# Loading k and q two heads to a transfer over all 128 partitions, with the first stage's engine orders rewritten: a three-layer kernel on one Trainium2 core

## The chip, the cores and the metric

One core of a Trainium2 chip. The metric is device time in microseconds (us), the median of several runs; lower is better. The engines are TensorE (PE, with its weight loads listed apart as PEld), VectorE (DVE), ScalarE (ACT), GpSimd (POOL) and SyncE (SP), whose queue issues nearly all DMAs.

## The reference, cut to what matters

Three layers follow one another: a Nystrom-style attention on q, k, v of shape (4, 8, 576, 64), then two feed-forward layers of width 2048 on the 2304 x 512 result.

```python
q_lm = q.reshape(B, H, 32, S // 32, D).mean(axis=3)      # 32 landmarks
k_lm = k.reshape(B, H, 32, S // 32, D).mean(axis=3)
A, Bm, C = sm(q, k_lm), sm(q_lm, k_lm), sm(q_lm, k)      # softmax of scaled scores
Z = Bm.T / (norm1(Bm) * norminf(Bm) + 1e-6)
for _ in range(6):
    Z = 2 * Z - Z @ Bm @ Z
x = A @ Z @ C @ v
h = x @ w_in;   x = (h * cos(h)) @ w_out                 # layer 2
h = x @ w_in2;  out = (max(h,0) + alpha*min(h,0)) @ w_out2
```

## The kernel before, in words

The work is cut into named operations. Each has a context and a number (`u0:20` is the twentieth operation of unit 0), a list of engines that may run it, and buffers from which the dependences follow. A long string, ORDER, lists all 3937 operations. `Plan.go` walks it and emits each operation on the engine behind the slash (`/A` ACT, `/V` DVE, `/G` POOL) or else on the first engine of its list. So ORDER is the program order of every engine: an engine runs its own entries strictly in turn, and an entry whose input is late holds all that stand behind it. No planner is in the file, only its result.

The contexts that matter here:

- `w`: filler matmuls on PE (L533), whose result is unused.
- `u0`, `u1` (batch 0) and `U2` to `U7` (batches 1 to 3): attention units of four heads, function `unit`. Operations 1 and 2 load k and q on SP, 3 loads v. In u0 and u1, 4 and 11 reorder k and q on ACT (L675), 5 to 10 and 12 to 17 transpose them in thirds on PE and copy each out (L688), 18 and 19 are the landmark sums on PE (L720), 20 and 21 scale them into `kq` (L727), 22 to 28 are scores, maximum and exponential of C, 29 to 32 transpose that and copy it out, 33 is C times v on PE (L816) and 36 scales it. 37 is the scores of A; 38 to 49 are their softmax and split, of which 41 (L850, subtract the maximum), 46 (L855, multiply by the reciprocal sum) and 49 (L555, low part) may go to POOL or DVE. From U4 on the landmarks come from two trees of five additions each on POOL (L742).
- `z0`, `z1`, `z2`: the 32 x 32 inverse iteration, a serial chain that alternates between PE (L936) and DVE (L953). It starts with L882, which needs `kq` of both units of its batch, and ends with `wt`. `z0:20` is the first step that also needs C v of both units (`u0:36`, `u1:36`).
- `v`, `V`: layer 2's input weights multiplied by `wt` (L999); `v0` needs `wt` and w_in blocks c0 to c3.
- `c0` to `c63`: conversion of a 128 x 512 weight block on DVE (L568, L570, L572) after its load (L562, SP). w_out blocks are then split in two on ACT (L552) and POOL or DVE (L555, operation 6). Raw blocks share three buffers.
- `t0` to `t127`: layer 2 in 128 ticks. `t:1` is six matmuls (L1043), 2 to 6 are ACT, DVE, ACT, DVE, ACT (the cosine, the product, its high part), 7 the low part on POOL or DVE (L1056), 8 to 11 twelve matmuls into the accumulators (L1068). `e` copies a finished group of accumulators out (L1092) on ACT or DVE.
- `b`, `s`, `y`, `o`: layer 3, by a Strassen scheme (L1357, L1438), from about 435 us on.

The subtractions of L552 to L556, L1056 and L850 run through the helper `sub` and so stand under L410 in the profile; copies stand under L405 and L407.

The k and q loads of u0 and u1 are two DMAs of 288 KB each, each into 64 of the 128 partitions (two heads side by side in a partition). Those of U2 to U7 are four DMAs of 144 KB each, one head into 64 partitions in pieces of 256 B. SP keeps at most eight DMAs under way: from the ninth on, each waits for the landing of an earlier one.

```python
for bb in range(2):                                         # L637, u0 and u1
    nc.sync.dma_start(
        out=t.t[64 * bb:64 * bb + 64].rearrange("p (h x) -> p h x", h=2),
        in_=src[b, 4 * c + 2 * bb:4 * c + 2 * bb + 2].rearrange("h (p r) d -> p h (r d)", r=NR))
```

Of the kernel before, what the change touches and what calls it, by code (L numbers as in the profile page):

```python
# [25 lines left out]
u1:14 w:11 u1:33 z0:15 z0:16 c2:2 U2:2 u1:35 u0:38 u0:39 c1:2 z0:18 u0:40 u1:36 u0:41/V z0:20 u1:12 w:12 u0:42
u1:15/A u1:13/A z0:21 c1:3 z0:22 U2:4 w:13 u1:16 c8:1 u1:17/A U2:6/A U2:5/A u0:43 u0:44 z0:19 c2:3 z0:23 c2:4 u0:45
u0:46/V z0:24 w:14 u1:37 c9:1 z0:25 c1:4 u0:47 z0:26 U2:14 u0:48 u1:39 u1:38 z0:27 u0:49/G u1:40 w:15 z0:28 z0:29
u1:41/V z0:30 U2:13 w:16 u1:42 U2:15/A c8:2 z0:31 u1:43 z0:32 z0:33/A U2:16/A z0:34/A u1:44 c8:3 c9:2 u1:45 c8:4 v0:1
w:17 U3:1 c3:5 c2:5 c11:1 v0:2 v0:4 u1:46/V v0:3 u1:47 v0:5 c9:3 u1:48 U2:10 c9:4 u1:49/V c11:2 U2:12/A U2:11/A U2:17  # L30
# [1486 lines left out]
```

## Time and profile before

| | us |
|---|---|
| timed runs, median (lowest, highest) | 830.67 (830.56, 831.22) |
| span of the profiled execution | 827.8 |
| median less span (what lies around the span) | 2.9 |
| first matmul of tick 0, last start of a tick's first matmul | 46.9, 431.8 |

The span is the time from the first to the last instruction of the profiled execution. Busy times of different engines overlap, so they don't add up to the span. A matmul counts as busy from its start to a modelled end, so a busy PE need not run at its full pace.

### The profile page before, as it was taken

What the parts mean: (1) busy time and instruction counts of PE and PEld (TensorE: products, weight loads), DVE (VectorE), ACT (ScalarE), POOL (GpSimd) and SP (SyncE); (2) the same over time, 40 slices, a digit from 0 to 9 for tenths busy, and PEclk for the clock granted to TensorE, in tenths of its full rate; (3) what the DMA queues carried; (4) which work ended last, traced back from release to release, by engine and by line L of the source; (5) the groups of instructions that cost most, each with busy time, mean ns of one, the idle gap of its engine ahead of it and who ended that gap; (6) DMA issues with size and microseconds to landing.
All of it is one profiled execution on the core that took longest, in us unless ns stands there. A gap on an engine that the chain in (4) does not pass through costs nothing.

```text
span 827.8 us, 16875 instructions
## 1 busy us (share of the span) xinstructions
PE 805.2 (97%) x6490; PEld 717.1 (87%) x6490; DVE 610.1 (74%) x1256; ACT 419.4 (51%) x943; POOL 192.9 (23%) x217
## 2 busy tenths in 40 slices
PE   8889999999999999999999999999999999999997
PEld 6567789988788898899999888989998989999886
DVE  3999799877886867889788998765565556456653
ACT  4468655778754557567764444522433244323231
POOL 0003312435530112036621113203400133000020
PEclk9999999999999999999999999999999999999999
DMA  9985466675666864454542422221031012120231
GB/s 222 217 236 155 132 164 209 164 173 115 137 206 210 259 199 151 146 181 168 168 146 87 131 90 66 78 85 39 13 102 51 9 57 83 48 62 14 81 111 26
DMA packets 87904, 103.34 MB, mean 125 GB/s; under 512 B 35856, under 2 KB 62992, under 8 KB 87824
## 3 DMA queue, kind: packets, MB, share of 16 engines
q1 hardware_dynamic: 87744, 102.14, 43.0%
q8 instruction: 51, 0.84, 0.4%
q14 instruction: 29, 0.24, 0.1%
q10 hardware_dynamic: 80, 0.13, 0.0%
HBM read 79.96 MB, written 22.28 MB: 124 GB/s over the span
## 4 chain that ended last, share of the span: by engine, by line
PE 70%; DVE 16%; ACT 5%; DMA 4%; issue 3%; POOL 0%; SPq 0%; DVEq 0%; ACTq 0%; POOLq 0%
PE acc L1438 20%; PE acc L1068 16%; PE h L1357 10%; PE h L1043 8%; PE x L1357 7%; DVE m L410 3%; DVE m L1050 1%; PE x L999 1%; DMA m<-in_moe_w_in_dram 1%; DVE m L572 1%; DVE m L570 1%; DVE m L1053 1%; DMA m<-wi2d 1%; PE x L1402 1%; PE h L1402 1%
## 5 line engine op out<-in xcount | busy, mean ns | idle before, releaser
L410 POOL TENSOR_TENSOR m<-m,m 128x288 fp32r<-128x288 f32 (+4 forms) x154 | 147.1, 968 | 580.0 <-ACT m L1055 213.5
L1068 PE MATMUL acc<-m,m 128*128 128x288 f32 x1536 | 235.4, 299 | 0.1
L1068 PEld LDWEIGHTS acc<-m,m 128*128 128x128 f32 x1536 | 211.2, 188 | 18.7 <-issue 12.7
L1438 PE MATMUL acc<-m,m 128*128 128x512 f32 x864 | 218.0, 392 | 0.6 <-ACT m L1426 0.2
L410 DVE TENSOR_TENSOR m<-m,m 128x512 fp32r<-128x512 f32 (+4 forms) x246 | 151.5, 636 | 48.3 <-ACT m L1426 18.1
L1438 PEld LDWEIGHTS acc<-m,m 128*128 128x128 f32 x864 | 154.1, 188 | 28.4 <-DVE m L410 1.3
L1043 PE MATMUL h<-m,m 128*128 128x288 f32 x768 | 125.0, 302 | 2.5 <-DVE m L1053 1.5
L1043 PEld LDWEIGHTS h<-m,m 128*128 128x128 f32 x768 | 108.5, 190 | 8.3 <-DVE m L1053 4.6
L1357 PE MATMUL h<-m,m 128*128 128x256 f32 x768 | 108.5, 282 | 0.3 <-ACT m L405 0.2
L1357 PEld LDWEIGHTS h<-m,m 128*128 128x128 f32 x768 | 102.6, 189 | 6.3 <-ACT m L405 0.7
L1426 ACT ACTIVATE m<-m 128x512 fp32r<-128x512 f32 (+1 forms) x80 | 46.1, 585 | 92.0 <-DVE m L1424 87.4
L1052 ACT ACTIVATE m<-m,quarter 128x288 f32<-128x288 f32 x128 | 67.0, 533 | 34.5 <-DVE m L1050 33.6
L1357 PE MATMUL x<-m,m 128*128 128x256 f32 x576 | 81.7, 283 | 0.3 <-DVE m L407 0.3
L1357 PEld LDWEIGHTS x<-m,m 128*128 128x128 f32 x576 | 76.5, 189 | 4.2 <-DVE m L407 0.6
L1048 ACT ACTIVATE m<-h 128x288 int32<-128x288 f32 x128 | 51.4, 406 | 47.3 <-PE h L1043 46.4
L405 ACT ACTIVATE m<-h 128x256 f32<-128x256 f32 (+2 forms) x86 | 33.5, 392 | 81.8 <-PE h L1357 65.0
L1050 DVE SCALAR_TENSOR_TENSOR m<-h,m 128x288 f32<-128x288 f32 x128 | 57.0, 450 | 23.8 <-ACT m L1048 23.4
L1055 ACT ACTIVATE m<-m 128x288 fp32r<-128x288 f32 x128 | 55.7, 440 | 30.5 <-DVE m L1053 25.6
L1053 DVE TENSOR_TENSOR m<-m,h 128x288 f32<-128x288 f32 x128 | 56.9, 448 | 12.9 <-ACT m L1052 10.1
L1189 ACT ACTIVATE m<-m 128x512 fp32r<-128x512 f32 x68 | 41.6, 625 | 29.2 <-PE h L1357 10.5
L1380 DVE TENSOR_TENSOR m<-h,m 128x512 f32<-128x512 f32 x32 | 21.9, 686 | 32.8 <-ACT m L405 21.8
L1424 DVE SCALAR_TENSOR_TENSOR m<-m,m 128x512 f32<-128x512 f32 x64 | 45.0, 718 | 0.8
(147 smaller groups left out, 768.0 us busy)
## 6 DMA issues: line engine op xcount, KB each, us to landing
m<-in_moe_w_in_dram SPq DMA_DIRECT2D x32, 512.0 KB, 5.6
m<-wi2d SPq DMA_DIRECT2D x56, 256.0 KB, 3.0
m<-in_moe_w_out_dram SPq DMA_DIRECT2D x24, 512.0 KB, 5.2
m<-w1d SPq DMA_DIRECT2D x32, 256.0 KB, 5.4
y1d<-m SPq DMA_DIRECT2D x24, 288.0 KB, 4.4
out_dram<-m SPq DMA_DIRECT2D x35, 128.0 KB, 2.8
w1d<-m SPq DMA_DIRECT2D x16, 256.0 KB, 5.6
wi2d<-m SPq DMA_DIRECT2D x16, 256.0 KB, 3.2
```

The costliest lines, as they stand in the source:

```text
L410: ENG[e].tensor_tensor(o, a, b, op=ALU.subtract)
L1043: nc.tensor.matmul(out=hp.t[:, 0:CW], lhsT=w_[:, js], rhs=x[:, cs], start=(i == 0), stop=(i == 5))
L1048: op(act(CW, True), lambda e: nc.scalar.activation(k_.t, hp.t[:, 0:CW], AF.Copy, scale=INV2PI, bias=0.25), r=[hp], w=[k_], target=T + 0.8)
L1050: op(dve(CW), lambda e: nc.vector.scalar_tensor_tensor(u.t, hp.t[:, 0:CW], INV2PI, k_.t, op0=ALU.mult, op1=ALU.subtract), r=[hp, k_], w=[u])
L1052: op(act(CW), lambda e: nc.scalar.activation(u.t, u.t, AF.Sin, scale=2.0 * math.pi, bias=quarter), rw=[u], aset="sin")
L1053: op(dve(CW), lambda e: nc.vector.tensor_tensor(hc.t, u.t, hp.t[:, 0:CW], op=ALU.mult), r=[hp, u], w=[hc], target=T + 2.6)
L1055: op(act(CW), lambda e: nc.scalar.activation(gh.t, hc.t, AF.Copy), r=[hc], w=[gh, gl])
L1068: nc.tensor.matmul(out=yg[o].t[:, 0:CW], lhsT=w_.t[:, sl], rhs=x.t, start=(j == ja and i == 0), stop=(j == jb and i == 2),)
L1357: nc.tensor.matmul(out=rv(k), lhsT=a_.t[:, p, c2, js], rhs=b_.t[:, q_, c2, 0:hw], start=(first and c2 == 0 and i == 0), stop=(c2 == 1 and ...
L1424: op(dve(w), lambda e, m_=m_, hv=hv: nc.vector.scalar_tensor_tensor(m_.t[:, 0:w], hv(), 0.0, m_.t[:, 0:w], op0=ALU.max, op1=ALU.add), r=hr ...
L1426: op(act(w), lambda e, m_=m_, gh=gh: nc.scalar.activation(gh.t[:, 0:w], m_.t[:, 0:w], AF.Copy), r=[m_], w=[gh, gl])
L1438: nc.tensor.matmul(out=ya[n][t].t, lhsT=gv(x_), rhs=r_.t, start=(st and k == 0), stop=(en and k == 2))
```

## The change

Loads: partition 64 * bb + s now holds heads 4c + bb and 4c + 2 + bb in place of 4c + 2bb and 4c + 2bb + 1. Two neighbouring heads lie end to end in DRAM, so one DMA now reads both and writes all 128 partitions. u0 and u1 keep two DMAs of 288 KB for each of k and q; U2 to U7 have two of 288 KB in place of four of 144 KB. v is loaded in the same number of pieces and sizes from other heads. The places that read `kq`, write scores, build `wt` and multiply it swap the roles of bb and hh; the number and shapes of their instructions stay.

```diff
-                    for bb in range(2):
+                    for hh in range(2):
                         nc.sync.dma_start(
-                            out=t.t[64 * bb:64 * bb + 64].rearrange("p (h x) -> p h x", h=2),
-                            in_=src[b, 4 * c + 2 * bb:4 * c + 2 * bb + 2].rearrange("h (p r) d -> p h (r d)", r=NR),
+                            out=t.t[:, hh * NR * D:(hh + 1) * NR * D],
+                            in_=src[b, 4 * c + 2 * hh:4 * c + 2 * hh + 2].rearrange("b (p r) d -> (b p) (r d)", r=NR),
...
-                    for bb in range(2):
-                        for hh in range(2):
-                            nc.sync.dma_start(
...
+                    for hh in range(2):
+                        nc.sync.dma_start(
+                            out=f32(t.t)[:, 0:2 * NR * D].rearrange("p (r h d) -> p r h d", h=2, d=D)[:, :, hh, :],
+                            in_=src[b, 4 * c + 2 * hh:4 * c + 2 * hh + 2].rearrange("b (p r) d -> (b p) r d", r=NR),
...
-                src = v[b, 4 * c + 2 * bb:4 * c + 2 * bb + 2].rearrange("h (p r) d -> p h r d", r=NR)
+                src = v[b, 4 * c + bb:4 * c + bb + 3:2].rearrange("h (p r) d -> p h r d", r=NR)
...
-                out=dst.t[64 * bb:64 * bb + 64, 0:n],
+                out=dst.t[64 * (bb ^ swap):64 * (bb ^ swap) + 64, 0:n],
...
-                nc.tensor.matmul(out=pw[bb].t[64 * hh:64 * hh + 64, i * M:i * M + M], lhsT=y.t[sl, i], rhs=bmv()[sl, i])
+                nc.tensor.matmul(out=pw[hh].t[64 * bb:64 * bb + 64, i * M:i * M + M], lhsT=y.t[sl, i], rhs=bmv()[sl, i])
```

ORDER has the same 3937 operations. Each engine's order is new up to about tick 95; from there on PE, ACT, DVE, POOL and SP keep their old order, layer 3 included. Many slashes vanish where they named the default engine. Queues at their start:

```
SP before:   u0:1 u0:2 c3:1 u1:1 u1:2 c0:1 u0:3 u1:3 c2:1 c1:1 U2:1 U2:2 c8:1 c9:1 U3:1
SP after:    u0:1 u0:2 u1:1 c2:1 u1:2 c3:1 c1:1 u0:3 c0:1 c9:1 u1:3 U2:1 c10:1 c11:1 U2:2 c4:1
DVE before:  c3:2 u0:8 u0:6 u0:20 u0:15 u0:23 u0:25 u0:26 c3:3 c3:4 u1:21 c0:2 z0:2
DVE after:   u0:10 u0:20 u0:21 u0:17 u0:13 c2:2 u0:23 u0:25 u0:26 c2:3 c2:4 u0:15 c3:2 c3:3 z0:2
POOL before: u0:49 t0:7 c6:6 t4:7 U2:34 ... t34:7 t35:7 c30:6 U4:16 U4:13 U5:16 U5:13 t44:7 t46:7 U6:16
POOL after:  u0:41 u1:41 u0:46 u1:46 u0:49 t0:7 t1:7 c5:6 t2:7 ... U4:16 t38:7 c29:6 t37:7 U4:13 t39:7 t40:7 t41:7 U4:36 U5:16 U5:13 t43:7
PE, both:    ... v0:1 w:17 U2:10 U2:17 t0:1 t1:1
```

Operations whose engine changes, by their place before or after a tick's first matmul in ORDER:

| moved | up to t32 | from t32 to t96 |
|---|---|---|
| L850 and L855 (576 wide), DVE to POOL | 6 | 4 |
| L555 (512 wide), DVE to POOL less back | 4 | 5 |
| L1056 (288 wide), DVE to POOL less back | 0 | 11 |
| L1092 (288 wide copies), ACT to DVE less back | 4 | 2 |
| L688 (384 wide copies), ACT to DVE less back | 1 | 0 |
| L702 (512 wide copies), ACT to DVE less back | 1 | 2 |
| L802 and L807 (512 and 128 wide copies), DVE to ACT | 1 | 4 |

## Rows read from the trace of the kernel before

**Rows 1.** The page's busy times: engine, busy us (share of the span), instructions.

```profile
span 827.8 us, 16875 instructions
PE 805.2 (97%) x6490; PEld 717.1 (87%) x6490; DVE 610.1 (74%) x1256; ACT 419.4 (51%) x943; POOL 192.9 (23%) x217
```

**Rows 2.** Windows: stretch, length; busy PE, PEld, DVE, ACT, POOL; clock; DMA share; GB/s.

```profile
10.00:20.00 10.00, 8.88 (x157) 6.48 (x159) 5.37 (x13) 5.67 (x13) 0.00 (x0) 1.00 1.07 246
20.00:40.00 20.00, 16.93 (x328) 11.47 (x324) 18.09 (x55) 8.26 (x19) 1.40 (x1) 1.00 1.04 217
100.00:160.00 60.00, 58.76 (x493) 52.35 (x493) 54.33 (x111) 38.56 (x90) 16.28 (x18) 1.00 0.65 183
160.00:240.00 80.00, 77.01 (x699) 67.17 (x698) 63.44 (x147) 58.84 (x127) 38.00 (x50) 1.00 0.65 153
435.00:828.00 393.00, 387.46 (x2427) 348.44 (x2425) 257.22 (x458) 141.51 (x314) 67.68 (x68) 1.00 0.21 65
```

**Rows 3.** Windows of L1043 alone (six matmuls a tick): busy PE, PEld; clock; DMA.

```profile
46.00:152.50 106.50, 33.02 (x193) 28.26 (x194) 0.98 0.63 179
152.50:355.00 202.50, 62.26 (x390) 54.26 (x389) 1.00 0.62 173
```

**Rows 4.** The chain that ended last: one undisturbed run of twelve tick matmuls.

```profile
158.76 1.59 PE acc L1068 x12
```

**Rows 5.** Timeline: start, length, operation, idle before it and who ended it.

```profile
10.15 0.43 DVE L568 TENSOR_SCALAR m<-m 128x512 int32<-128x512 int32 x1 [7.47 <-DMA m<-in_moe_w_in_dram]
19.31 0.42 PE L882 MATMUL h<-m 64*32 64x32 f32 x16
27.88 0.87 PE L936 MATMUL h<-m 32*32 32x96 f32 x16
41.33 1.33 PE L999 MATMUL x<-m,m 64*32 64x512 f32 x16 [0.60 <-ACT m L731]
46.89 3.03 PE L1043 MATMUL h<-m,m 128*128 128x288 f32 x12
```

**Rows 6.** Windows, all engines, while the first loads arrive.

```profile
8.00:10.00 2.00, 2.00 (x44) 1.71 (x41) 0.00 (x0) 0.49 (x1) 0.00 (x0) 1.00 1.02 316
11.00:15.00 4.00, 2.88 (x38) 1.69 (x34) 1.73 (x5) 2.49 (x3) 0.00 (x0) 1.00 1.05 230
15.00:16.00 1.00, 1.00 (x9) 0.61 (x9) 0.43 (x2) 0.00 (x0) 0.00 (x0) 1.00 0.98 378
```

**Rows 7.** Waits of PE, 0 to 60 us: us in total, times, longest.

```profile
PE x L720 <- DMA m<-in_q_dram: 0.3, 1, 0.3
```

**Rows 8.** Lines by form, DVE, 0 to 60 us: count, busy us, mean ns.

```profile
L572 DVE SCALAR_TENSOR_TENSOR m<-m,m 128x512 int32<-128x512 int32 x10 | 6.8, 680 | 0.1
L855 DVE TENSOR_TENSOR m<-m 128x576 f32<-128x576 f32 x2 | 1.5, 750 | 0.0
L410 DVE TENSOR_TENSOR m<-m,m 128x512 fp32r<-128x512 f32 x2 | 1.4, 686 | 0.2 <-ACT m L552 0.2
L410 DVE TENSOR_TENSOR m<-m,m 128x288 fp32r<-128x288 f32 x1 | 0.5, 451 | 0.0
```

**Rows 9.** Lines by form, POOL, whole span: count, busy us, mean ns.

```profile
L410 POOL TENSOR_TENSOR m<-m,m 128x288 fp32r<-128x288 f32 x64 | 56.2, 882 | 216.2 <-ACT m L1055 213.5 <-PE acc L1068 1.2 <-DVE m L568 1.2
L410 POOL TENSOR_TENSOR m<-m,m 128x512 fp32r<-128x512 f32 x28 | 38.6, 1380 | 225.4 <-ACT m L1426 136.1 <-ACT m L1189 58.4 <-ACT m L552 18.8
L410 POOL TENSOR_TENSOR m<-m 128x576 f32<-128x576 f32 x3 | 3.5, 1160 | 8.6 <-DVE m L849 5.5 <-PE x L882 3.0
```

**Rows 10.** Lines by form, DVE, 160 to 240 us, where POOL is half busy.

```profile
L572 DVE SCALAR_TENSOR_TENSOR m<-m,m 128x512 int32<-128x512 int32 x4 | 3.8, 957 | 0.0
L410 DVE TENSOR_TENSOR m<-m,m 128x512 fp32r<-128x512 f32 x2 | 1.7, 836 | 0.7 <-ACT m L552 0.7
```

**Rows 11.** Lines, POOL, whole span: the additions of the eight landmark trees.

```profile
L742 POOL TENSOR_TENSOR m<-m 128x512 f32<-128x512 f32 (+3 forms) x32 | 24.7, 774 | 17.9 <-ACT m L405 14.2 <-ACT m L1048 1.9
...
L742 POOL TENSOR_TENSOR m<-m,m 128x128 f32<-128x128 f32 x8 | 4.1, 515 | 0.6
```

More of the change, by code (lines that the diff above doesn't have):

```diff
@@ L26 @@
[L26 to L30, printed above, removed]
@@ new lines @@
+t39:6 U4:13 t39:7 t36:11 t37:11 t40:5 U4:21 U4:22 U4:23 U4:24 t38:8 t37:10 t38:10 t41:1 t36:9 t37:9 t38:11 t42:3 t42:4
+t41:2 U4:15 U4:14 t41:3 U4:32 U4:34 U4:33 U4:35 t38:9 t39:11 t39:8 t40:6 t40:7 t41:4 t41:5 t41:6 t42:5 U5:7 U4:29 U5:9/V
+t39:10 t44:1 e39:6 U5:8 t41:7 U4:25 U4:26 t44:2 U4:27 U4:36 t39:9 t43:1 e39:7 U5:10 t40:8 U4:28 t42:6 e39:2 e39:3 U4:30
+t44:3 U5:11 U5:12 t44:4 t42:7/V t41:8 t40:9 t42:8 e39:8 c19:5 t43:2 t44:5 t43:3 U4:31 t43:4 V0:7 U5:4 t43:5 U5:5/V t41:9
+t45:1 t40:10 c25:5 U5:16 U5:6/V U5:17/A U4:37 U5:18 t46:1 U5:19 U5:20 U5:21 U5:22 t45:2 U5:13 t43:6 U5:23 t40:11 U4:38
@@ new lines @@
+t45:3 t41:10 t42:10 t41:11 t42:11 U5:14 U5:24 U5:15/A t46:2 t44:6 U5:32 U5:33 t43:7 t44:7 t45:4 U4:39 U5:34 U5:29 t46:3
+U6:2 t43:8 t43:10 t44:10 U5:25 t45:5 U4:40 t46:4 t46:5 U5:27/V t47:1 t45:6 U5:26 U6:7 U5:30 U5:35 U6:1 e39:4 t47:2 U6:8
+U6:9/V V0:8 U5:3 e47:5 t44:8 t42:9 U6:10 t45:7 U6:12/V t46:6 t48:1 U6:11/V U5:28 t45:8 t48:2 t47:3 t47:4 t47:5 U5:31
+t45:10 U7:1 e47:1 U6:4 t48:3 U7:2 c17:5 c32:1 U4:41 U4:42 t43:9 t44:9 t45:9 U6:16 U6:18 U6:17 U6:5 U6:6 t48:4 t46:7
+U6:13 t43:11 U6:19 U5:36/V U5:37 U6:21 t46:9 t49:1 t44:11 U6:20 U6:22 t48:5 t47:6 U6:24 U6:23 U4:43 t50:1 U7:4 U6:29
@@ L244 @@
+b37:5 b36:7 b37:9 b37:6/G b36:8 b37:10 s72:10/V b37:11 b36:13 b38:1 b36:14 b37:7 b38:2 b37:12 b38:3 b38:9 b38:4 b38:5
+b39:1 b37:13 b38:6/G b39:3 b38:10 b39:4 b37:8 b39:2 b39:5 b38:11 b38:7 b38:12 b37:14 b39:6 b39:9 b38:13 b39:10 b38:8
+b39:11 b39:12 b39:7 b38:14 b39:13 b39:8 b39:14 b39:16 b39:17 b39:15 b39:19 b39:18
 """
@@ L727, in kw @@
                 def kw(e, sl=sl, hh=hh):
-                    o = kq[p][sl, :, 1:3] if c and hh == 0 else kq[p][sl, :, 0:4:3] if c else kq[p][sl, :, hh:4:2]
+                    o = kq[p][sl, :, hh:4:2]
                     i = pt.t[sl, 0:256].rearrange("p (x y b m) -> p y b x m", x=2, y=2, b=2)[:, 0]
@@ L762, in unit, with scores @@
                     op([dve2(64), act(64)], kw, r=[lt], w=[kqb[p][i]])
-        def scores(dst, ch, which, t, bb, pp):
+        def scores(dst, ch, which, t, bb, pp, swap=0):
             n = 64 * (CH[ch][1] - CH[ch][0])
             nc.tensor.matmul(
-                out=dst.t[64 * bb:64 * bb + 64, 0:n],
+                out=dst.t[64 * (bb ^ swap):64 * (bb ^ swap) + 64, 0:n],
                 lhsT=kq[pp][:, bb, 2 * which:2 * which + 2].rearrange("p h m -> p (h m)"),
@@ L842, in asc @@
                     for bb in range(2):
-                        scores(sa[x], x, 0, qt, bb, p)
+                        scores(sa[x], x, 0, qt, bb, p, c)
             if ch == 0:
@@ L968, in z_path, with put @@
             wt[b] = sb("wt", [P, 2, 2, M])
-            for bb in range(2):
-                def put(e, bb=bb, w_=wt[b], k_=k_):
-                    copy(e, w_.t[:, :, bb], pw[bb].t[:, 2 * k_ * M:2 * (k_ + 1) * M].rearrange("p (i m) -> p i m", i=2))
-                op([dve(64), act(64, True)], put, r=[pw[bb]], w=[wt[b]], target=tz)
+            for hh in range(2):
+                def put(e, hh=hh, w_=wt[b], k_=k_):
+                    copy(e, w_.t[:, :, hh], pw[hh].t[:, 2 * k_ * M:2 * (k_ + 1) * M].rearrange("p (i m) -> p i m", i=2))
+                op([dve(64), act(64, True)], put, r=[pw[hh]], w=[wt[b]], target=tz)
     vv, vload = {}, {}
```

430 lines of the change are left out of this document (203 added, 227 removed).

## The prediction

> **What bounds the kernel now.** I read the page's busy times first, then the windows by stage, then the timeline of the first 50 us. PE is busy 97% of the span [rows 1], so the whole can gain only where PE waits or runs fillers. The windows say where that is. In layer 3 (435 us on, an order that the change keeps) PE is busy 387.5 of 393 us: nothing is to be had there. From 20 to 160 us it is DVE that is nearly always busy, 18.1 of 20 us and 54.3 of 60 us, with POOL at 1.4 and 16.3 us [rows 2]. "Busy" hides waits inside PE's own instructions, so I compare paces. A matmul of a tick takes 1.59 / 12 = 0.1325 us undisturbed [rows 4], a tick of 18 thus 2.39 us. Tick matmuls L1043 number 193 from 46 to 152.5 us, 32 ticks at 3.3 us each, and 390 in the next 202.5 us, 65 ticks at 3.1 us [rows 3]. PE has other work there too, but a good part of the surplus is waiting. So stage one goes at DVE's pace until about tick 32, and by PE and the length of each tick's chain after it.
>
> The start is bound by the loads. DVE stands idle until 10.15 us, 7.47 us of it for a weight load; the inverse iteration starts at 19.31, `v0` at 41.33, tick 0 at 46.89 us [rows 5]. From 10 to 20 us DVE works 5.4 us, from 20 to 40 us 18.1 [rows 2].
>
> **Part 1, the loads of u0 and u1.** Eight loads of 288 KB (294,912 B) each. While k and q go to 64 partitions, the DMA engines are full (share 1.05) and move 230 GB/s: 1.28 us a load. Where a weight block to all 128 partitions is under way they move 316 GB/s over two microseconds, and 378 in one [rows 6]. No row shows a k load over 128 partitions, so I bound it: 1.28 us (no gain) to 0.78 us (378), and take 316 GB/s, the longer stretch with the same partitions: 0.93 us. Eight loads save 8 x 0.35 = 2.8 us at the last, bounds 0 and 4.0. One weight block still stands between them on SP, so the inverse iteration could start some 3 us earlier.
>
> What is late next is DVE. From the new order, with durations of rows, DVE has 29.3 us of work ahead of `v0` against 29.2 before, but 20.1 against 15.8 ahead of `z0:20`, which is at 27.88 us now [rows 5]. So the chain gains little until that join and more behind it. DVE's first block, now at 10.15, lands after four such loads: 1.4 us earlier. Of its 6.5 us of idle time from 10 to 40 us [rows 2] the new queue, which has three weight blocks loaded ahead of v, fills some, say 1.4 us: `v0` near 38.5 instead of 41.33. Ahead of tick 0 DVE then has 0.7 us more than before, of which I charge half: 2.5 us gained at tick 0, bounds 0 and 4.0. [...]
>
> **Part 2, the loads of U2 to U7.** 24 DMAs fewer on SP, and larger ones. PE waited for one of these once in the first 60 us, 0.3 us [rows 7]; other work covers the rest, so I count nothing, bounds 0 and a gain of 0.3 us. If the cover goes (a U3 load behind `c8` in SP's new queue), the wait falls on `t2`, since PE takes U3's landmarks ahead of it.
>
> **Part 3, work moved off DVE.** Up to tick 32: six 576-wide operations at 0.75 and four 512-wide at 0.686 go to POOL [rows 8], 7.2 us. Back to DVE come four accumulator copies, 0.45 each by the row nearest in size, one 384-wide copy, some 0.5 by the same row, and smaller ones: 2.6 us. Net 4.6 us. POOL takes 6 x 1.16 + 4 x 1.38 = 12.5 us more [rows 9]. That is not free: beside a half-busy POOL the conversions on DVE take longer, L572 0.957 instead of 0.680 and the 512-wide subtraction 0.836 instead of 0.686 us [rows 8, 10]. Those six instructions lose 1.4 us against 38 us of POOL [rows 2], 0.04 us per us; with the other lines that read two tiles I take 0.1, so 1.2 us given back, bounds 0.5 and 5.1 (0.04; and 0.41, an estimate: twice the 0.28 that an L572 lost on the mean, over a POOL operation of 1.38). DVE sets the pace here, so the net 3.4 us counts in full, bounds -0.5 and 4.1.
>
> From tick 32 to 96: four 576-wide, five 512-wide and eleven 288-wide (0.451) leave DVE, 11.4 us; copies take back some 2 us net; POOL gets 21.2 us more, worth 2.1 us. Net 7.3 us. But DVE is busy only 63.4 of 80 us there [rows 2], so I count a quarter, about the share by which a tick's 3.1 us lie above 2.39: 1.8 us, bounds 0 and 7.3.
>
> Exchanged roles of bb and hh, the v loads and the scores change no count and no shape: nothing. Fillers stay 17.
>
> **The sum.** 2.5 + 3.4 + 1.8 = 7.7 us. The profiled span is 827.8 us, and the median 830.67 lies 2.9 us above it; taking that as constant, 830.67 - 7.7 = 823.0 us. About 0.2%, 1.7 us, is what a measurement of this kernel can tell from no change.
>
> [...]
>
> **Rivals.**
>
> *It gains more* (816 us, chance 0.17): loads at the fast bound and DVE's relief counting fully after tick 32: 4.0 + 3.4 + 7.3 = 14.7 us. For it: the ticks' 3.1 us against 2.39 leave PE room. Against it: from 160 to 240 us ACT, too, is busy 58.8 of 80 us [rows 2].
>
> *Only the loads count* (828.2, chance 0.15, a third of that within 0.2%): each tick's chain from h to product, not DVE's load, sets the pace. For it: PE counts as busy 77 of 80 us from 160 to 240 us [rows 2].
>
> *The loads don't go faster* (825.5, chance 0.07): the rate belongs to the piece size or the DRAM side, and 230 GB/s stays. Then only 5.2 us remain. Against it: 316 GB/s a moment later, from the same DRAM [rows 6].
>
> *POOL comes late, and PE waits for it* (837.4, chance 0.14): before, ticks 36 to 43 kept their low parts on DVE while the trees of U4 and U5 ran on POOL. Now `t43:7` stands behind `U4:36` (576 wide, 1.16 us) and two trees, 28.8 / 8 = 3.6 us each [rows 11]: 8.4 us late, plus 0.88 of its own. PE's order leaves a tick in that part at least 43 matmuls, 5.7 us, between its `t:1` and its first use of that result. So up to 3.6 us are lost per unit, 14.4 in four, and 14.4 - 7.7 makes it 6.7 us slower. It decides from 1.9 us per unit. Against it: most of these ticks have 9 to 14 us of other PE work in between.
>
> *DVE blocked one for one* (836, chance 0.03): a POOL operation holds up whatever DVE runs, for its whole length: 12.5 - 4.6 - 2.5 = 5.4 us lost. The rows of L572 speak against it: it grew by 0.28 us beside operations of about a microsecond.
>
> **How the numbers follow.** The forecast's own case (820 to 827) has 0.44. Faster by over 0.2%: 0.44 + 0.17 + 0.10 + 0.07, less 0.02 for the forecast falling short: 0.76. Slower: 0.14 + 0.03, less 0.02 for a POOL wait that only eats the gain: 0.15. Within 0.2%: 0.09. The range reaches from 815 (the large gain) to 831.5 (no change, and the smallest losses); what lies outside is most of the slower cases and little below.
>
> **What would show it.** Right: k and q of u0 and u1 arriving at over 300 GB/s; DVE's first real work before 9 us; the inverse iteration's L882 near 16 us and L999 near 38.5; tick 0 near 44.4; tick 32 some 6 us earlier; POOL busier by about 34 us and DVE less by about 14; layer 3 as long as before. Wrong: a rate that stays near 230 GB/s; tick 32 at its old time though DVE has less to do; PE waiting for POOL around ticks 37 to 50; DVE's conversions stretched by more than they shrank in number; a lead at tick 32 that is gone by tick 96.

## The result, and the profile after

The changed kernel takes 815.34 us in the median (814.85 to 816.34), the kernel before beside it 830.62: ratio 0.9822, 95% interval 0.9805 to 0.984. It is 15.3 us faster where 7.7 were forecast. Line numbers in the changed kernel are 15 lower from L675 on (L1043 is now L1028, L1068 is L1053), and 13 lower up to L638 (L410 is now L397); the other kernels have a few lines more or less.

The page, busy times of the kernel after, as in [rows 1]:

```profile
span 813.0 us, 16870 instructions
PE 799.3 (98%) x6490; PEld 716.1 (88%) x6490; DVE 594.9 (73%) x1234; ACT 413.0 (51%) x930; POOL 226.8 (28%) x250
```

DVE lost 15.2 us of work and POOL gained 33.9, close to the forecast's 14 and 34: the moves themselves were counted rightly. The span fell by 827.8 - 813.0 = 14.8 us.

Where it fell is read from the windows of the kernel after, with the columns of [rows 2]:

```profile
10.00:20.00 10.00, 9.92 (x143) 7.75 (x142) 9.55 (x27) 5.12 (x13) 0.00 (x0) 1.00 0.97 289
20.00:40.00 20.00, 17.30 (x346) 11.42 (x342) 17.74 (x51) 8.45 (x21) 7.24 (x5) 1.00 0.98 233
...
160.00:240.00 80.00, 79.70 (x884) 69.18 (x884) 60.95 (x155) 55.03 (x118) 45.37 (x59) 1.00 0.70 183
420.00:813.00 393.00, 387.66 (x2427) 348.51 (x2425) 257.41 (x458) 141.38 (x314) 68.27 (x68) 1.00 0.22 65
```

Layer 3 is as long as before, 393 us. The clearest change is the third busy time of the first line, DVE's: it works 9.55 of 10 us between 10 and 20, where it worked 5.37. From 160 to 240 us PE is busy 79.70 of 80 us in place of 77.01. (The number of matmuls there, 884 against 699, says little, since the two kernels are at different places of the work there; of the tick matmuls L1043 alone it is 127 against 126.)

The loads, in windows of one microsecond (last number: GB/s). In the trace a packet of u0's or u1's k or q has 2,304 B and one of a weight block 4,096 B, so the stretches can be told apart. Before, with only k and q of u0 on their way:

```profile
4.00:5.00 1.00, 1.00 (x5) 1.00 (x5) 0.00 (x0) 0.00 (x0) 0.00 (x0) 1.00 1.12 221
5.00:6.00 1.00, 0.87 (x5) 0.58 (x3) 0.00 (x0) 0.00 (x0) 0.00 (x0) 1.00 1.00 230
6.00:7.00 1.00, 0.00 (x0) 0.00 (x0) 0.00 (x0) 0.97 (x1) 0.00 (x0) 1.00 1.05 226
```

After, with only k and q under way (3 to 6 us), and then with a weight block nearly alone (11 to 12):

```profile
3.00:4.00 1.00, 1.00 (x4) 1.00 (x4) 0.00 (x0) 0.00 (x0) 0.00 (x0) 1.00 1.12 394
4.00:5.00 1.00, 1.00 (x5) 1.00 (x5) 0.00 (x0) 0.54 (x1) 0.00 (x0) 1.00 1.03 327
5.00:6.00 1.00, 1.00 (x7) 0.56 (x7) 0.00 (x0) 0.62 (x1) 0.00 (x0) 1.00 0.93 336
...
11.00:12.00 1.00, 1.00 (x16) 0.73 (x14) 1.00 (x3) 0.00 (x0) 0.00 (x0) 1.00 1.00 408
```

The DMA share is 0.93 to 1.12 in all of them, so the engines were full, and the same engines move k and q with 327 to 394 GB/s (353 over the three microseconds) into 128 partitions against 221 to 230 into 64: 0.84 us a load in place of 1.28 to 1.33. What this is worth is best read from the last of the eight loads, with one weight block ahead of it in either queue. It lands at 12.12 us in place of 15.25, 3.1 us sooner. (The two halves of one tensor land 0.72 to 0.76 us apart, before 1.22 to 1.34, but the gaps between tensors are larger.)

The milestones, in the timeline of the kernel after (columns of [rows 5]):

```profile
8.75 0.56 DVE L394 COPY m<-h 128x384 f32<-128x384 f32 x1 [6.07 <-PE h L671]
...
15.49 0.33 PE L867 MATMUL h<-m 64*32 64x32 f32 x16
...
36.91 1.09 PE L984 MATMUL x<-m,m 64*32 64x512 f32 x16 [0.40 <-ACT m L392]
...
41.23 1.85 PE L1028 MATMUL h<-m,m 128*128 128x288 f32 x12
...
139.88 0.96 PE L1028 MATMUL h<-m,m 128*128 128x288 f32 x6
```

The last of these is tick 32's first matmul; before, it is the second line of this stretch of the timeline:

```profile
151.76 0.83 PE L1068 MATMUL acc<-m,m 128*128 128x288 f32 x5
152.42 0.83 PE L1043 MATMUL h<-m,m 128*128 128x288 f32 x5
```

Against [rows 5] the inverse iteration starts 19.31 - 15.49 = 3.8 us earlier, `v0` 4.4, tick 0 5.66. Tick 32 is 12.5 us earlier, the last start of an L1043 matmul 14.9 (431.8 to 416.9). So over a third of the gain is made ahead of tick 0, nearly half from there to tick 32, and little after it.

The stretch from tick 0 to tick 32, all engines, first before and then after:

```profile
46.85:152.35 105.50, 101.46 (x987) 87.82 (x986) 96.64 (x220) 70.92 (x160) 26.39 (x27) 0.99 0.63 180
```

```profile
41.20:139.85 98.65, 96.82 (x981) 85.17 (x980) 90.59 (x208) 69.26 (x156) 33.97 (x33) 1.00 0.63 179
```

About as many matmuls of PE, some 985, take 6.85 us less. DVE has 6.05 us less to do in it, and its busy share is the same, 96.64 / 105.5 = 0.916 and 90.59 / 98.65 = 0.918.

Last, the clock. Before, windows around the first matmul of tick 0 (eighth number: granted clock):

```profile
43.00:44.00 1.00, 0.18 (x2) 0.00 (x0) 0.69 (x2) 0.76 (x2) 0.00 (x0) 1.00 0.67 172
44.00:45.00 1.00, 0.44 (x2) 0.20 (x2) 1.00 (x2) 0.28 (x1) 0.00 (x0) 1.00 0.81 266
45.00:46.00 1.00, 0.59 (x5) 0.40 (x7) 0.97 (x3) 0.73 (x3) 0.00 (x0) 1.00 0.48 193
46.00:49.40 3.40, 3.40 (x16) 2.66 (x13) 3.33 (x8) 0.78 (x3) 0.00 (x0) 0.51 0.57 155
```

After, the same place in the work:

```profile
38.00:39.00 1.00, 0.53 (x3) 0.23 (x2) 0.42 (x2) 0.96 (x2) 1.00 (x1) 1.00 0.70 233
39.00:40.00 1.00, 0.44 (x2) 0.20 (x2) 1.00 (x3) 0.70 (x2) 0.35 (x1) 1.00 0.98 311
40.00:41.00 1.00, 0.89 (x8) 0.52 (x8) 1.00 (x3) 0.28 (x1) 0.00 (x0) 1.00 1.28 283
```

Before, PE was busy 0.18, 0.44 and 0.59 us in three microseconds, and the granted clock was 0.51 over the 3.4 us behind them. After, it was busy 0.53, 0.44 and 0.89, and the granted clock was 1.00 in all three and is 1.0 over the whole span. Tick 0's first twelve matmuls take 1.85 us in place of 3.03. That holds for these two executions. The granted clock over the whole span is 0.998 in the execution of the kernel before that is shown here, and 1.0 in four of its 18 executions beside the last runs below; those four took 830.9 to 831.4 us, the others 828.3 to 832.7. So it isn't shown that the fall to 0.51 costs anything in the end.

### The profile page after: what moved, and what is told of

Same layout as the page of the kernel before. It is cut to its first block, busy times and chain, and to the rows that moved or that the text cites. A ratio compares the mean times of both kernels' runs of the same rounds, so it can differ in the third digit from the quotient of the medians.

```text
span 813.0 us, 16870 instructions
## 1 busy us (share of the span) xinstructions
PE 799.3 (98%) x6490; PEld 716.1 (88%) x6490; DVE 594.9 (73%) x1234; ACT 413.0 (51%) x930; POOL 226.8 (28%) x250
## 4 chain that ended last, share of the span: by engine, by line
PE 68%; DVE 18%; ACT 5%; issue 4%; DMA 3%; POOL 1%; SPq 0%; DVEq 0%; ACTq 0%; POOLq 0%
PE acc L1423 19%; PE acc L1053 15%; PE h L1342 9%; PE h L1028 8%; PE x L1342 7%; DVE m L397 3%; DVE m L1035 1%; DVE m L559 1%; DVE m L1406 1%; DVE m L1038 1%; PE x L751 1%; DVE m L1409 1%; ACT m L1037 1%; DVE m L1365 1%; DMA wi2d<-m 1%
## 5 line engine op out<-in xcount | busy, mean ns | idle before, releaser
L397 POOL TENSOR_TENSOR m<-m,m 128x288 fp32r<-128x288 f32 (+4 forms) x176 | 169.7, 976 | 514.2 <-ACT m L1411 178.9
L1053 PE MATMUL acc<-m,m 128*128 128x288 f32 x1536 | 234.1, 298 | 0.2
L1053 PEld LDWEIGHTS acc<-m,m 128*128 128x128 f32 x1536 | 211.0, 188 | 15.6 <-issue 9.9
L397 DVE TENSOR_TENSOR m<-m,m 128x512 fp32r<-128x512 f32 (+4 forms) x224 | 139.4, 643 | 43.7 <-ACT m L1411 18.1
L1028 PE MATMUL h<-m,m 128*128 128x288 f32 x768 | 124.6, 299 | 2.4 <-DVE m L1038 2.0
L1028 PEld LDWEIGHTS h<-m,m 128*128 128x128 f32 x768 | 107.8, 188 | 9.4 <-DVE m L1038 6.0
L1037 ACT ACTIVATE m<-m,quarter 128x288 f32<-128x288 f32 x128 | 67.4, 534 | 37.7 <-DVE m L1035 36.7
```

Of the source, the lines that this page charges most:

```text
L397: ENG[e].tensor_tensor(o, a, b, op=ALU.subtract)
L1028: nc.tensor.matmul(out=hp.t[:, 0:CW], lhsT=w_[:, js], rhs=x[:, cs], start=(i == 0), stop=(i == 5))
L1037: op(act(CW), lambda e: nc.scalar.activation(u.t, u.t, AF.Sin, scale=2.0 * math.pi, bias=quarter), rw=[u], aset="sin")
L1053: nc.tensor.matmul(out=yg[o].t[:, 0:CW], lhsT=w_.t[:, sl], rhs=x.t, start=(j == ja and i == 0), stop=(j == jb and i == 2),)
```

## The experiments

Three parts were changed at once: loads, sequence and engines. My theory after the result was that each gives its own share; the rivals were that the loads carry it, that the engine moves carry it, and that the parts work only together. Each run was timed beside the kernel before on its own chip; "gain" is that kernel's median there less the run's (829.98 for the new loads with the old ORDER, all old pieces, the old engines and the new order to tick 0; 829.5 for the old pieces of u0 and u1, the new engines in the old sequence, the softmax steps and the old order to tick 32; 830.13 for the other four). The intervals of the ratios are worth some 1.1 to 2.3 us either way. "Tick 0" and "tick 32" are the starts of ACT's first operation of these ticks in the trace.

| run | time, us | gain | ratio, 95% interval | tick 0 | tick 32 | between |
|---|---|---|---|---|---|---|
| before | 830.62 | | | 49.1 | 153.5 | 104.4 |
| the change | 815.34 | 15.3 | 0.9822 [0.9805, 0.984] | 43.2 | 140.9 | 97.7 |
| new loads, old ORDER | 830.24 | -0.3 | 1.0003 [0.9988, 1.0018] | 48.1 | 154.3 | 106.2 |
| all old pieces | 822.37 | 7.6 | 0.992 [0.9896, 0.9944] | 49.7 | 147.5 | 97.8 |
| old pieces, u0 and u1 | 820.73 | 8.8 | 0.9891 [0.9869, 0.9913] | 47.7 | 145.4 | 97.7 |
| old pieces, U2 to U7 | 818.11 | 12.0 | 0.9858 [0.983, 0.9886] | 43.4 | 141.4 | 98.0 |
| new sequence, old engines | 837.47 | -7.5 | 1.0098 [1.0074, 1.0123] | 47.8 | 152.1 | 104.3 |
| old sequence, new engines | 850.01 | -20.5 | 1.0252 [1.0233, 1.0271] | 51.8 | 169.0 | 117.2 |
| low parts on old engines | 835.03 | -4.9 | 1.0057 [1.0038, 1.0077] | 43.0 | 146.4 | 103.4 |
| softmax steps on DVE | 820.8 | 8.7 | 0.9902 [0.9887, 0.9917] | 46.5 | 146.3 | 99.8 |
| four more on POOL | 818.26 | 11.9 | 0.9848 [0.9825, 0.987] | 43.7 | 143.6 | 99.9 |
| new order to tick 0 | 822.51 | 7.5 | 0.9918 [0.9895, 0.9942] | 42.4 | 146.8 | 104.4 |
| old order to tick 32 | 827.97 | 1.5 | 0.9977 [0.9964, 0.999] | 48.5 | 153.1 | 104.6 |
| old order to tick 0 | 829.12 | 1.0 | 0.9983 [0.9972, 0.9995] | 51.5 | 154.2 | 102.7 |

### The loads alone, in the old ORDER

```diff
 ORDER = """
-u0:1 u0:2 u0:4 w:2 w:9 u0:11 w:7 w:6 w:8 w:10 u0:18 u0:7 u0:5 u0:9 u1:1 c2:1
+w:7 w:5 w:6 w:4 w:9 w:1 w:10 u0:1 u0:2 c3:1 u1:1 u0:4 u0:7 u0:5 u0:9 w:3
...
```

> The changed kernel's loads and head pairing under the old order and the old engines. Theory A: the loads alone bring some 2 to 4 us, 826.5 to 828.5 us, with DVE's first weight block earlier than 10.15 us. Theory B: under 1 us, near 830 us, because DVE's old queue is full behind the start. Theory C: within 1 us of the kernel before, since the old sequence waits at the same places.

Nothing is gained: 830.24. Its timeline and windows:

```profile
45.51 2.10 PE L1032 MATMUL h<-m,m 128*128 128x288 f32 x12
```

```profile
48.00:50.00 2.00, 1.31 (x8) 0.84 (x8) 1.93 (x5) 1.98 (x6) 0.00 (x0) 1.00 1.17 268
50.00:54.00 4.00, 2.63 (x38) 2.51 (x39) 3.72 (x9) 3.63 (x8) 1.07 (x1) 0.58 0.75 208
54.00:58.00 4.00, 4.00 (x46) 3.61 (x45) 1.85 (x5) 1.41 (x4) 0.00 (x0) 0.57 0.91 284
```

Tick 0's first matmul comes 46.89 - 45.51 = 1.4 us earlier. But PE, earlier in its old queue, now pauses a little after that (it is busy 1.31 of 2 us from 48 us on), and the granted clock is 0.58 and 0.57 over the two windows of 4 us that follow, where the kernel before had 0.51 over one of 3.4 us: 1.4 us of lead are gone by tick 32. The last of the eight loads lands at 11.20 us there, 4.0 us sooner than before, so the loads do go faster; the old queue makes nothing of it. That the clock is what takes the lead back is argued from these windows, not shown by a run.

### The old pieces in the new order

```diff
-                    for hh in range(2):
+                    for bb in range(2):
                         nc.sync.dma_start(
-                            out=t.t[:, hh * NR * D:(hh + 1) * NR * D],
-                            in_=src[b, 4 * c + 2 * hh:4 * c + 2 * hh + 2].rearrange("b (p r) d -> (b p) (r d)", r=NR),
+                            out=t.t[64 * bb:64 * bb + 64].rearrange("p (h x) -> p h x", h=2),
+                            in_=src[b, 4 * c + bb:4 * c + bb + 3:2].rearrange("h (p r) d -> p h (r d)", r=NR),
...
-                    for hh in range(2):
-                        nc.sync.dma_start(
+                    for bb in range(2):
+                        for hh in range(2):
+                            nc.sync.dma_start(
...
```

The pairing of heads stays the new one; only the partitions that one DMA fills go back. Three runs: all of it, the first half (u0, u1) and the second (U2 to U7).

> The changed kernel, with its order and engines, but k and q again loaded in pieces to 64 partitions (two of 288 KB for u0 and u1, four of 144 KB from U2 on); same heads in the same places. Theory A (the faster loads open the start, and the rest follows from it): the eight first loads land 0.57 us apart slower, the last 4.6 us later, tick 0 comes 3 to 5 us later and the time is 818 to 820 us. Theory B (the work moved from DVE to POOL makes the gain, DVE has slack for late loads): under 1 us, 815 to 816.5 us. Theory C (the new sequence makes it, but was laid out for these loads): more than the loads' own 4.6 us, over 820 us.

> The changed kernel with only the k and q loads of u0 and u1 in pieces to 64 partitions; U2 to U7 keep their 128-partition loads. If the first eight loads are what the old pieces cost: tick 0 again 5 to 7 us late, 820 to 823 us. If half of it were the loads from U2 on: tick 0 under 4 us late, 817 to 819 us. A half-clock stretch near 27 us with 3 us lost there, as with all old pieces, would show again if the pause that precedes it comes from the first loads.

> Only U2 to U7 load k and q as four pieces of 144 KB into 64 partitions again; u0, u1, the order and the engines are the changed kernel's. Theory A (the loads of U2 to U7 are worth the difference between the run with all old pieces, 822.4, and the run with old pieces for u0 and u1 alone, 820.7): 816.5 to 817.5 us, with the start of tick 0 within 1 us of the changed kernel's. Rival B (their price was one of the half-clock stretch that fell on the run with all old pieces; by themselves they are covered): 815.0 to 815.8. Rival C (in the new order U2's loads stand ahead of weight blocks, so slower pieces delay the ticks' weights): 818 or more, the loss growing from tick 0 to tick 16.

Here the same loads are worth 815.34 against 822.37, about 7 us, more than the loads' own delay, as theory C had it. The timelines give tick 0 with all old pieces, and with old pieces for u0 and u1 alone:

```profile
47.78 1.85 PE L1030 MATMUL h<-m,m 128*128 128x288 f32 x12
```

```profile
45.70 1.84 PE L1028 MATMUL h<-m,m 128*128 128x288 f32 x12
```

So u0's and u1's eight loads are worth 45.70 - 41.23 = 4.5 us at tick 0. The last of them lands 3.3 us later with old pieces (15.38 against 12.12), and what stands behind them on SP is later still: `c1` 3.9 us (20.29 against 16.39), the v loads of u0 4.2 to 4.5. With all old pieces the new order starts tick 0 at 47.78, later than the old order's 46.89: that order is written for loads of the new speed. Part of this may be the clock, which was 0.50 from 28 to 34 us of the run with all old pieces, after two microseconds in which PE was busy 0.10 and 0.30 us; its windows:

```profile
24.00:25.00 1.00, 0.10 (x1) 0.00 (x0) 0.97 (x7) 0.28 (x1) 0.00 (x0) 1.00 1.11 205
25.00:26.00 1.00, 0.30 (x1) 0.11 (x1) 0.96 (x6) 1.00 (x6) 0.00 (x0) 1.00 1.22 190
...
28.00:34.00 6.00, 5.38 (x70) 3.19 (x67) 2.81 (x7) 0.69 (x2) 1.66 (x1) 0.50 0.90 241
```

With old pieces for u0 and u1 alone, PE is busy 0.16 and 0.30 us from 24 to 26 us, nearly the same, and the granted clock is 1.00 from 24 to 36 us. So about 2 of the 7 us (47.78 - 45.70) go along with a clock of 0.50 in one of two runs with nearly equal pauses; that they come from it isn't shown by a run. From tick 0 to 32 these runs keep the full gain, 97.7 and 97.8 us.

U2 to U7 were costed at nothing. Alone they cost 1.4 us of span (814.4) and, in the medians, 818.11, with the ratio's interval overlapping the changed kernel's. Tick 0 is where it was (43.4), as two of the three theories had it, and the third's growth from tick 0 to 16 isn't there; the loss comes between ticks 32 and 56. PE's waits from 140 to 240 us in that run:

```profile
PE x L686 <- DMA m<-in_q_dram: 0.6, 1, 0.6
PE x L686 <- DMA m<-in_k_dram: 0.6, 1, 0.6
PE x L803 <- DMA m<-in_v_dram: 0.5, 1, 0.5
```

The changed kernel has no DMA among its waits there. So the slow pieces of the later units do come late in the new order, 1.7 us of waits in all, and the larger ones remove that. The size stays open: 1.4 us by the spans, 2.8 by the medians, 3.3 by the gains. The stretch is also a touchy one. From tick 32 to 56 this run takes 86.8 us in place of 84.3, and the run with the softmax steps on DVE, which has the new loads, takes 86.9.

### Sequence without engines, engines without sequence

```diff
 ORDER = """
 u0:1 u0:2 u0:4 ...
-u1:2 u0:10/V u0:20 u0:6 u0:21 u0:12
+u1:2 u0:10 u0:20 u0:6/V u0:21/A u0:12
...
```

This is the new sequence with every operation on its old engine. The other run is the reverse: the old sequence, each operation on its new engine.

> The changed kernel's loads and sequence, but every operation of the first stage on the engine that it had before (27 low parts, ten softmax steps, nine block splits back on DVE, and so on). Theory B: most of the 15 us is lost, over 823 us; 4 to 6 of it by tick 32. Theory A and C: tick 0 stays within 1 us of the changed kernel and the time grows by 2 to 5 us, 817 to 820 us.

> The changed kernel's loads and engines, in the old sequence. Theory B (the engines alone make ticks 0 to 32 shorter): these ticks take 98 to 100 us instead of 104.4 and the time is 820 to 824 us. Theory D (engines and sequence only work together: an operation moved to POOL must also stand early enough there and leave DVE a place that the new sequence uses): over 827 us, tick 32 within 2 us of the kernel before.

Neither stands alone: 837.47 and 850.01, both slower than before. With the old engines the new sequence takes 104.3 us from tick 0 to 32, just the old pace, and is 11.2 us behind the changed kernel at tick 32, where theory B had 4 to 6. With the new engines the old sequence takes 117.2. A part of it shows in SP's waits (75 to 115 us in this run and the kernel before, 40 to 125 us in the changed kernel), for the store of a finished accumulator group, whose copy went from ACT to DVE. The run with new engines in the old sequence:

```profile
SPq L1083 <- DVE m L397: 25.0, 1, 25.0
```

The kernel before:

```profile
SPq L1095 <- ACT m L405: 20.1, 1, 20.1
```

The kernel after:

```profile
SPq L1080 <- DVE m L394: 10.2, 1, 10.2
```

And the windows of the run with new engines in the old sequence:

```profile
80.00:100.00 20.00, 17.04 (x172) 13.69 (x169) 16.74 (x43) 12.76 (x29) 10.31 (x10) 1.00 0.01 5
100.00:120.00 20.00, 16.63 (x189) 13.59 (x187) 10.85 (x26) 7.69 (x16) 2.74 (x3) 0.91 0.42 136
```

SP waits 25 us for one copy on DVE, and behind it no weight moves: 5 GB/s over 20 us. In the next 20 us DVE is busy only 10.85 us. That the missing weights emptied DVE is argued from these lines, not shown by a run. The kernel before has such a wait too, 20.1 us with its DMAs as still (0 to 6 GB/s from 76 to 92 us), so only the 5 us on top are new. Another part is DVE work that lasts longer beside POOL, 9.5 us of it, counted below under "Four more low parts on POOL".

### Which engine moves count

```diff
 ORDER = """
...
-t3:4 t1:7 c5:6 U2:28
+t3:4 t1:7/V c5:6/V U2:28
...
-c6:5 t2:7 t4:4
+c6:5 t2:7/V t4:4
...
```

So for all 56 low parts (L555, L1056) whose engine the change moved; the other run puts the ten softmax steps back:

```diff
 ORDER = """
...
-z0:20 u0:41 w:12
+z0:20 u0:41/V w:12
...
-z0:30 u0:46 U2:14
+z0:30 u0:46/V U2:14
...
```

> The changed kernel with every low part (t:7, and the low halves of weights and of the softmax results) on its engine of before; the sequence, the loads, the ten softmax steps and the copies stay changed. Theory A (the new sequence has room for POOL's longer operations and needs DVE free; all engine moves together are worth 22 us here, the softmax steps 5.5): the low parts carry most of the rest, 825 to 832 us, lost tick by tick from 0 to 64. Rival B (the copies between ACT and DVE carry it): 816 to 820. Rival C (low parts on POOL only lengthen each tick's chain): under 815.

> The changed kernel with only its ten softmax steps of width 576 (L850, L855 of the kernel before; four of them ahead of tick 0) back on DVE, in the new sequence. If these steps are what frees DVE at the start: tick 0 comes 3 to 5 us later, near 47 us, as with all old engines (47.8), and the time is 820 to 824 us. If it was the low parts: tick 0 stays within 1 us of 43.2 and the time within 2 us of the changed kernel, 815 to 817 us.

The low parts carry most: without their move the time is 835.03, slightly over the 832 at which the expectation ended, and all of it is lost among the ticks: 103.4 us from 0 to 32, and from 32 to 64 123.1 against 114.4.

The ten softmax steps are worth 5.5 us (6.6 by the gains), 3.3 of them ahead of tick 0, where four run. The rival with the copies has no run of its own. The one by which low parts on POOL only lengthen each tick's chain falls, since it had the time under 815.

### Four more low parts on POOL

```diff
 ORDER = """
...
-c5:2 c4:6/V t1:6
+c5:2 c4:6 t1:6
...
-U3:5/V c6:6/V t6:3
+U3:5/V c6:6 t6:3
...
-c13:5 c12:6/V t9:1
+c13:5 c12:6 t9:1
-z1:17 c13:6/V z1:15
+z1:17 c13:6 z1:15
...
```

> The changed kernel with four more 512-wide low halves of weights (c4, c6, c12, c13, between ticks 0 and 8) on POOL in place of DVE, 4 x 0.69 = 2.7 us less on DVE where it is busiest. Theory A (up to tick 32 DVE's work sets the pace and a POOL microsecond costs DVE nothing): 812.5 to 814.5 us. Rival B (POOL's strict order makes later low parts late, each by the 1.4 us of the operation put ahead of them): 815.5 to 818. Rival C (DVE no longer sets the pace in the new order): 815.0 to 815.6.

818.26, 2.9 us slower than the changed kernel, with intervals that overlap; 2.2 us of it lie between ticks 0 and 32 (99.9 against 97.7). Theory A has two halves, and one of them falls: here POOL's time did cost DVE something. From tick 0 to tick 32 (by the table's times), this run and then the changed kernel:

```profile
43.70:143.60 99.90, 96.93 (x975) 84.40 (x974) 92.32 (x203) 68.27 (x154) 39.70 (x37) 1.00 0.62 178
```

```profile
43.20:140.90 97.70, 95.87 (x975) 84.30 (x973) 89.68 (x207) 68.29 (x154) 33.97 (x33) 1.00 0.63 183
```

DVE has four instructions fewer, 2.7 us of work by their usual length, and yet is busy 2.64 us longer. Two of its instructions in this run:

```profile
59.65 1.74 DVE L562 SCALAR_TENSOR_TENSOR m<-m,m 128x512 int32<-128x512 int32 x1
...
73.09 1.21 DVE L916 TENSOR_SCALAR m<-m 128x2 f32<-128x2 f32 x1
```

The usual length of the first is 0.68 us and of the second 0.16. Beside the first, POOL ran one of its 512-wide subtractions from 59.56 to 60.84 us, beside the second one from 73.00 to 74.27. In the traces of the kernels before and after this is so throughout: over the whole span 75 and 64 DVE instructions took over 0.1 us more than the median of their form, and every one of them ran while POOL ran one. The sums of what such instructions took too long, from tick 0 to tick 32:

| run | ticks 0 to 32, us | DVE busy, us (share) | of it too long, us (instructions) | POOL busy, us |
|---|---|---|---|---|
| before | 104.4 | 95.2 (0.91) | 2.5 (9) | 26.8 |
| the change | 97.7 | 89.7 (0.92) | 2.7 (6) | 34.0 |
| four more on POOL | 99.9 | 92.3 (0.92) | 7.1 (13) | 39.7 |
| softmax steps on DVE | 99.8 | 92.7 (0.93) | 4.5 (8) | 31.5 |
| low parts on old engines | 103.4 | 95.1 (0.92) | 6.8 (14) | 30.6 |
| new sequence, old engines | 104.3 | 94.1 (0.90) | 6.0 (12) | 28.5 |
| old sequence, new engines | 117.2 | 98.9 (0.84) | 9.5 (17) | 37.7 |

Two things follow. DVE's busy share is nearly the same in all but the last run, where the DMAs stand still for 20 us; so this stretch goes at DVE's pace in the new order too, as far as shares can show it. And the loss beside POOL doesn't follow from how long POOL works: the changed kernel loses 2.7 us beside 34 us of POOL, the new sequence with the old engines 6.0 beside 28.5. It may depend on which instructions meet, which no run shows by itself. The changed order and engines lose little here (2.7 us), as those of before do (2.5), and the mixed pairings lose more (4.5 to 9.5). Rival B, a late low part on POOL, has only one wait of PE for POOL to show, 0.3 us. No run was faster than the changed kernel.

### How far the new order reaches

```diff
 ORDER = """
-w:7 w:5 w:6 w:4 w:9 w:1 w:10 u0:1 u0:2 c3:1 u1:1 ... U2:17 c10:1 c4:1 t0:1 U3:2 U2:18
+u0:1 u0:2 u0:4 w:2 w:9 u0:11 w:7 w:6 w:8 w:10 ... U2:21 U2:22 c11:4 t0:1 c8:1 c8:2
...
```

This takes the new order and engines up to tick 0's first matmul and the old ones behind it. Two others start with the old order, up to tick 32 and up to tick 0.

> The new loads; everything that stands before tick 0's first matmul in the new order in the new order and engines, all the rest in the old sequence and on the old engines. Theory A: the lead of tick 0, 5.9 us, is kept to the end or grows: 822 to 825 us. Theory B: half of it is lost again in the DVE-bound ticks, 826 to 829 us. Theory C: the lead is kept to tick 32 (5 to 6 us) and no further gain comes, 824 to 826 us.

> The new loads; everything up to tick 32's first matmul in the old sequence and on the old engines, all the rest in the new sequence and on the new engines. If the new order gains after tick 32 by itself (it gained 2 to 3 us there in the changed kernel): 827 to 828.5 us. If the later gain only follows from the earlier lead: 829.5 to 831 us.

> The order and the engines of before up to tick 0, then those of the changed kernel; the loads are the changed kernel's. Theory A (the start and the ticks are two separate gains: new up to tick 0 alone gave 7.5 us, and the ticks after it 7.2 more): 822 to 824 us, tick 0 where it was before and the ticks up to 32 quicker by 6 us. Rival B (the ticks' gain needs the early start, since weights and units must lie ready for it): 827 to 831.

New up to tick 0 gives 7.5 us, and the ticks then run at the old pace, 104.4 us to tick 32: the lead is kept (822.51, as theory A had it). New from tick 32 on alone gives 1.5 us. What is left, 15.3 - 7.5 - 1.5 = 6.3 us, is the ticks 0 to 32, where the traces of before and after differ by 6.7.

The last run can't confirm that from the other side. Its splice makes a later weight block (c19) overwrite the converted block c0 ahead of c0's last use, so the store of c0 waits for that block and writes it in c0's place. SP's waits from 40 to 125 us:

```profile
SPq L585 <- DVE m L562: 11.2, 1, 11.2
```

Windows of the same run:

```profile
48.00:50.00 2.00, 0.00 (x0) 0.00 (x0) 1.86 (x5) 0.00 (x0) 0.00 (x0) 1.00 1.15 265
50.00:54.00 4.00, 2.83 (x26) 2.50 (x28) 2.98 (x7) 3.33 (x8) 0.00 (x0) 0.56 0.63 147
...
104.00:108.00 4.00, 3.91 (x30) 3.68 (x29) 3.25 (x8) 2.19 (x6) 1.57 (x2) 1.00 0.01 4
...
112.00:116.00 4.00, 2.23 (x15) 2.18 (x15) 2.85 (x7) 0.83 (x2) 0.00 (x0) 0.92 0.82 331
```

The DMAs stand still up to 108 us, and PE is busy 2.23 of 4 us after that; at 48 to 50 us PE has nothing at all, and the granted clock is 0.56 in the 4 us behind it. Neither of the two kernels shows the like (from 100 to 120 us PE is busy 19.08 and 19.70 of 20). The run is inconclusive, and whether the ticks' gain needs the early start is open.

## Why the prediction came out as it did

The time lies in the range, though only just inside its lower end (815), and the direction was right; the gain is twice what was forecast, and the large-gain rival's 816 is nearer than the forecast's 823.0. By the spans, the 14.8 us split into 5.66 ahead of tick 0, 1.18 for the clock (3.03 - 1.85), 5.67 for the rest of ticks 0 to 32 (6.85 - 1.18) and 2.3 after it. The forecast had 2.5, no term for the clock, 3.4 and 1.8.

**Part 1, the price of a load: right.** "I ... take 316 GB/s ...: 0.93 us", and 2.8 us for the eight. It was 0.84 us by the stretch with k and q alone, and 3.1 us at the last landing; with the new loads under the old ORDER it was 4.0, the far bound. The 316 was a mean over weight blocks and 64-partition loads, so that it came out near is luck in part. Over 128 partitions k and q stay below a weight block (327 to 394 GB/s against 408).

**Part 1, what is late next: half right, too small.** "The chain gains little until that join and more behind it": DVE's first real work came at 8.75 us and the inverse iteration at 15.49, as forecast (before 9, near 16), but `v0` gained 4.4 us where 2.8 were forecast. The fill of DVE's idle time was taken as 1.4 us plus 1.4; from 10 to 20 us DVE worked 4.2 us more. What stands behind the eight loads gains too: with old pieces `c1` and v of u0 land 3.9 to 4.5 us later, and the forecast had no price for v. The charge of half of 0.7 us ahead of tick 0 was wrong in sign: from `v0` to tick 0 it takes 4.32 us in place of 5.56. And the step gave the loads a price of their own; the run with the old ORDER shows that without the new queue they have none at the end.

**The clock: not in the sum.** PE's queue around `v0` and tick 0 is the same in both orders but its pause is not: 0.53, 0.44 and 0.89 us of work in the three microseconds ahead of tick 0 against 0.18, 0.44 and 0.59, and a granted clock of 1.00 behind them against 0.51, in the executions shown. As executions of the kernel before with a clock of 1.0 over the whole span are not shorter (830.9 to 831.4 us against 828.3 to 832.7), the 1.18 us of the split above is a share of two traces, not of the medians.

**Part 2: too small.** Costed at nothing; worth 1.4 to 3.3 us in this order, more than the bound of 0.3. That bound came from a view of the first 60 us [rows 7], and all but 0.3 us of these waits come after 140.

**Part 3, up to tick 32: right mechanism, two sizes off.** "DVE sets the pace here, so the net 3.4 us counts in full." The stretch shrank by 5.67 us besides the clock, as DVE's work in it did, 6.05, at the same busy share. The net count of 4.6 missed that four of the six softmax steps (3.0 us) run ahead of tick 0, and that the new queue does more of DVE's other work there: DVE is busy 29.52 us ahead of tick 0 in place of 30.14, though those four steps are gone. The charge of 1.2 us for POOL's work was the other size. Some DVE instructions did take longer beside POOL (nine before and six after in this stretch), but in this order that cost next to nothing more: 2.7 us in place of 2.5. DVE's last step of a conversion (L572 of the kernel before; count, busy us, mean ns), from tick 0 to tick 32, before:

```profile
L572 DVE SCALAR_TENSOR_TENSOR m<-m,m 128x512 int32<-128x512 int32 x24 | 16.8, 702 | 0.1
```

after:

```profile
L559 DVE SCALAR_TENSOR_TENSOR m<-m,m 128x512 int32<-128x512 int32 x22 | 16.4, 747 | 0.3
```

and with four more low parts on POOL:

```profile
L562 DVE SCALAR_TENSOR_TENSOR m<-m,m 128x512 int32<-128x512 int32 x22 | 17.2, 780 | 0.3
```

A price per microsecond of POOL, as the prediction took it, can't describe this: 7 us more of POOL cost 0.2 us in the one order, and 6 us more on top of it cost 4.4. A single instruction lost more than the 0.28 us that the prediction read from the mean: L562 above took 1.74 us in place of 0.68 beside a POOL subtraction of 1.28 us. Over all of POOL's time the changed kernel shows far less: 2.7 us beside 34.0.

**Part 3, after tick 32: the size is near, the reason open.** A quarter of 7.3 us was counted, 1.8; 2.3 came, and 1.5 by the run that is old up to there. The later loads, priced at nothing, are worth about as much in the same stretch, and no run tells the two apart.

**The rivals.** *POOL comes late* did not happen around ticks 37 to 50; PE's waits from 140 to 240 us hold a single one of 0.2 us, for DVE. Old sequence with new engines loses 20.5 us, but it isn't shown that late low parts do it. *The loads don't go faster* is refuted by 327 to 394 GB/s, and *DVE blocked one for one* by the 2.7 us beside 34 us of POOL. *Only the loads count* is refuted twice: alone they give nothing, and without them the new order gives 7.6 us.

What the prediction lacked as a whole is that its parts don't add. New engines without the new sequence -20.5, new sequence without the new engines -7.5 (both with the new loads), loads alone -0.3, all together 15.3 us.

## What to carry to other kernels

Fill all 128 partitions with one DMA where two neighbouring blocks lie end to end in memory (here 327 to 394 GB/s in place of 221 to 230), and then rewrite the queues behind it: the faster load paid nothing in the old order and some 7 us in one written for it. Read the speed of a transfer from a stretch in which only that kind is under way, since a mixed window gives a mean, and what it is worth from the landing of the last one. Cost an order and its engine assignment as one thing; a move that relieves the busiest engine can be worse than none (here 850.01 us with the new engines in the old sequence, the kernel before 829.5 beside it). When work goes from DVE to POOL, compare DVE's busy time before and after with what was taken off it: in the run with four more low parts, 2.7 us of work were taken off it and it was busy 2.6 us longer.
